# One token block instead of two goes through the row gather, and ScalarE's share of that work is issued later

## The chip, the cores and the metric

The kernel runs on one core of one Trainium2 chip. The metric is the device time of one execution in microseconds (us). TensorE (PE in the profile), VectorE (DVE), ScalarE (ACT) and GpSimd (POOL) each run their own instructions strictly in order, and SyncE (SP) issues most of the DMAs, in order too. An instruction waits for the semaphores of what it needs; everything behind it on its engine waits with it. GpSimd issues the indirect DMAs and the DMAs that add to their target.

## The reference, cut to what matters

2048 tokens of 512 numbers are normalised, and the result is the input plus two branches: a Fourier mix over both axes, and a layer of 4096 small experts. For each token and each of 32 heads the second branch picks 2 experts out of 4096 (by two rounds of top-2 over scores against the keys), weighs them by a softmax, and sums the value rows:

```python
x = A_x
xn = _layernorm(x, axis=-1)
...
g = _softmax(top_s, axis=-1)
ue = u[top_e]
ve = v[top_e]
act = _gelu(jnp.einsum("nd,nhkd->nhk", xf, ue))
out = jnp.einsum("nhk,nhk,nhkd->nd", g, act, ve)
...
return x + _A_ref(xn, ...) + _B_ref(xn, ...)
```

So a token has 64 slots (32 heads, 2 experts each). A slot costs one dot product of the token with a row of `u`, a gelu, a product with the gate, and one scaled row of `v`.

## The kernel before

The tokens are 16 blocks of 128. A first part of the program does the Fourier mix, all the scores and the routing; it ends at about 450 us, with the expert numbers `eix` and gates `gts` of the last `NS` blocks on the chip. What follows is the expert stage, and the change lies there. Two ways of doing a block run side by side in it.

**Dense blocks** (`NB` = 16 − `NS` of them). All 4096 experts are computed for the block. `u_part(b, cg)` makes 128 x 512 products with `u` in PSUM (tile `z`, 48 matmuls, two banks of the tag `pb` in turn), and ScalarE takes each out with a gelu into `act` (L936). `g_mm` builds on TensorE the matrix `g` of gates (zero for experts that were not picked) out of one-hot tiles `L` and `R` that VectorE writes (L959, L964, L967). `w_part` multiplies `act` by `g` on VectorE into a tile `w` (L979), ScalarE rounds it to a 16-bit half (L983) and VectorE takes the rest as a second half (L984). `v_part` multiplies the halves with `v` (L991), eight steps `cg` of 12 matmuls for one block, and `finish` adds the sum to `y` on VectorE (L1006), where the Fourier branch and the input already are (`add_x`), and stores it.

**Row blocks** (the last `NS`). For each slot an indirect DMA fetches a row of `u` and a row of `v` for each of the 128 tokens into one tile `ga` (`fetch`, L1017, 512 KB). `dot` multiplies the `u` half by the token on VectorE and sums (L1037); ScalarE does the gelu and the gate on the 128 sums (tile `za`, L1038 and L1039) and, in `gain`, scales the `v` half (L1045); GpSimd adds it to the block's sum `ov` (L1046). There are `NS` x 64 slots, in order.

The loop is over the dense blocks: eight steps of `v_part(b)`, then eight steps of `u_part(b+2)` while there is such a block. I call one such pair a period: the V phase and the U phase. `w_part` and `g_mm` of the next blocks are placed at fixed steps by the small tables `vw`, `vg`, `uw` and `ug`. After every step from block 1 on, `pick` issues the next pieces of the row work, spread evenly: `picks` is the list dot, gain, dot, gain, and so on, over `turns` steps. In the same steps `paced` issues two streams of checks that the first part could not finish: `fit` (ScalarE takes the sum of magnitudes of a tile) and `compare` or `compare_w` (a DMA, several subtractions on VectorE called `diff`, and two sums of magnitudes on ScalarE called `judge`). A function appended to `later` is issued one step on. `verdict` reduces the checks over the partitions with two `PARTITION_ALL_REDUCE` on GpSimd and sets a flag that decides whether a slower path runs afterwards.

Within a phase the order on each engine is that of issue, as the recording layer schedules it; `follow` and `hold` only place an instruction behind a matmul in that order, they add no wait.

Of the kernel before, what the change touches and what calls it, by code (L numbers as in the profile page):

```python
# [19 lines left out]
P = 128  # L20
# [12 lines left out]
NS = 2  # L33
# [3 lines left out]
def tile_fnet_peer(ctx, tc, x, ca, cb, c5, wt, wf, wr, wq, kt, ut, vn, uv, out):  # L37
# [515 lines left out]
    def part_b(safe, stS, stP, stE, xt, u_sb, cmp_p):  # L553
# [161 lines left out]
        def compare(n, at=None):  # L715
# [188 lines left out]
        BT = [blk_tiles(b) for b in range(2)]  # L904
# [4 lines left out]
        BUFS = 3  # L909
        AHEAD = BUFS - 1  # L910
# [63 lines left out]
        def w_part(b, tg):  # L974
            act, _ = ACT[b]
            ts = slice(tg * TG, (tg + 1) * TG)
            p = GP.pop((b, tg))
            w = bp.tile([P, NC, TG], F32, tag="w", name=f"w{b}_{tg}", bufs=WB)
            nc.vector.scalar_tensor_tensor(w, act[:, :, ts], fw,  # L979
                                           p.rearrange("p h (n c) -> p c (h n)", c=NC),  # L980
                                           op0=ALU.mult, op1=ALU.mult)
            w16 = parts(b)[:, :, ts]
            nc.scalar.activation(w16[..., 0], w, AF.Copy)  # L983
            nc.vector.tensor_tensor(w16[..., 1], w, w16[..., 0], op=ALU.subtract)  # L984
# [36 lines left out]
        def dot(n, s):  # L1021
            if s == 0:
                b = NB + n
                xs = bp.tile([P, 2 * D], F32, tag="ga", name=f"xs_{n}", bufs=BUFS)[:, :D]
                T["x"] = pc(f"px{n}")
                T["z"] = bp.tile([P, N], F32, tag="za", name=f"za{n}", bufs=1)
                T["o"] = o = bp.tile([P, D], F32, tag="ov", name=f"ov{n}", bufs=1)
                nc.sync.dma_start(xs, x[b // 4, b % 4])
                nc.sync.dma_start(o, y_d[b])
                nc.gpsimd.dma_start(o, x[b // 4, b % 4], accum_op=ALU.add)  # L1030
                norm(T["x"], xs, b)
                if n == 0:
                    for _ in range(AHEAD):
                        fetch()
            t = T[n, s][:, :D]
            z = T["z"][:, s:s + 1]
            nc.vector.scalar_tensor_tensor(t, t, 1.0, T["x"], op0=ALU.mult, op1=ALU.mult, accum_out=z)  # L1037
            nc.scalar.activation(z, z, AF.Gelu_apprx_tanh)  # L1038
            nc.scalar.activation(z, z, AF.Copy, scale=gts[:, n].rearrange("p k h -> p (k h)")[:, s:s + 1])  # L1039
            fetch()  # L1040

        def gain(n, s):
            o = T["o"]
            t = T.pop((n, s))[:, D:]
            nc.scalar.activation(t, t, AF.Copy, scale=T["z"][:, s:s + 1])  # L1045
            nc.gpsimd.tensor_tensor(o, o, t, op=ALU.add)  # L1046
            if s == N - 1:
                b = NB + n
                nc.sync.dma_start(out[b * P:(b + 1) * P], o)
# [17 lines left out]
        def compare_w(n):  # L1067
# [35 lines left out]
            later.append(lambda mm: nc.scalar.activation(f, f, AF.Abs, accum_out=chk[:, n:n + 1]))  # L1103

        def fit(n):

            if n < NW:
                t = bp.tile([P, 2 * D], F32, tag="w", name=f"fit{n}", bufs=WB)
                nc.sync.dma_start(t.rearrange("p (h k) -> p h k", h=2), wq[1 + n // 4, n % 4 // 2, n % 2])
                later.append(lambda mm: nc.scalar.activation(t, t, AF.Abs, accum_out=fits[:, n:n + 1]))  # L1110
# [5 lines left out]
            nc.scalar.activation(t, src, AF.Abs, accum_out=fits[:, n:n + 1])  # L1116
# [75 lines left out]
        for cg in range(8):  # L1192
            u_part(1, cg)
            if cg % 2 == 0:
                w_part(0, cg // 2)
# [4 lines left out]
        last = list(range(V2, 16))  # L1200
        for b in range(NB):
            pv = pc(f"v{b}")
            if b + 2 < NB:
                vw, vg, uw, ug = {0: 0, 4: 1}, {2: 2, 6: 3}, {0: 2, 4: 3}, {2: 0, 6: 1}
            else:
                vw, vg = {0: 0, 2: 1, 4: 2, 6: 3}, {0: 2, 3: 3}
            for cg in range(8):
# [3 lines left out]
                mm = v_part(b, pv, cg)  # L1211
                if b + 1 < NB and cg in vw:
                    w_part(b + 1, vw[cg])
# [21 lines left out]
            for cg in range(8 if b + 2 < NB else 0):  # L1235
                mm = u_part(b + 2, cg)
                if cg in uw:
                    w_part(b + 1, uw[cg])
# [150 lines left out]
```

## Time and profile before

| what | us |
|---|---|
| median of 3 runs (1172.79 to 1180.67) | 1174.48 |
| the profiled execution | 1180.07 |
| its span | 1178.2 |
| expert stage up to the first V phase | 450.0 to 503.7 |
| twelve periods (V phase of block b, U phase of block b+2) | 503.7 to 1114.0 |
| V phases of blocks 12 and 13, and the end | 1114.0 to 1178.2 |
| VectorE, ScalarE, GpSimd busy in the whole span | 984.5, 731.5, 658.1 |
| TensorE busy in the whole span | 1085.4 |

A period starts with the first `v` matmul of its block. Those stand in the trace's order in time at 503.74, 554.02, 602.21, 649.16, 701.17, 749.39, 796.99, 847.99, 905.16, 960.14, 1014.21, 1062.20 and 1113.97 us. In a group's row the last column is the time in which the engine sat idle just ahead of such instructions, with what ended the wait behind the arrow.

### The profile page before, as it was taken

The page shows a single profiled execution, that of the slowest core. Times are in us where ns is not written, and L with a number is a line of the kernel's source. Part 1 is how long each engine was busy: PE and PEld are TensorE (multiplying, and loading weights), DVE is VectorE, ACT ScalarE, POOL GpSimd, SP SyncE. Part 2 cuts the span into 40 slices and gives each one's busy share as a digit, 9 for nine tenths or more (in the row PEclk, how much of TensorE's full clock was granted, in tenths as well). Part 3 has the DMA queues.
Part 4 walks back from the last instruction along what each step waited for, and adds up shares of the span by engine and source line. Part 5 has one row for each costly group of instructions (what it writes and reads, how often), then busy time and mean ns, then how long its engine had stood idle before and what let it go on. Part 6 is the DMA issues. An engine that isn't in the chain of part 4 may idle for free. (4 is left out here: it accounts for less than half of the span.)

```text
span 1178.2 us, 28689 instructions
## 1 busy us (share of the span) xinstructions
PE 1085.4 (92%) x11070; PEld 710.4 (60%) x11070; DVE 984.5 (84%) x2886; ACT 731.5 (62%) x1429; POOL 658.1 (56%) x570
## 2 busy tenths in 40 slices
PE   6899999999999999999999989999879797999885
PEld 4355555444444447958668676786748576786732
DVE  7878888797987998889898978789688987889861
ACT  3575567787877874457666657666555665675550
POOL 0021748779878771246557556666565655566542
PEclk9799999999999999999999999999998998999998
DMA  8265236253542421345765656666654656565541
GB/s 309 77 218 177 92 124 214 93 180 124 166 161 85 144 97 60 103 139 171 214 201 169 215 182 209 185 191 199 198 169 167 194 164 204 168 203 173 162 117 48
DMA packets 82418, 190.44 MB, mean 162 GB/s; under 512 B 10070, under 2 KB 26845, under 8 KB 82272
## 3 DMA queue, kind: packets, MB, share of 16 engines
q1 hardware_dynamic: 61378, 117.20, 29.7%
q0 software_dynamic: 20736, 71.31, 20.4%
q8 instruction: 88, 1.44, 0.5%
q14 instruction: 58, 0.48, 0.1%
q10 hardware_dynamic: 158, 0.01, 0.0%
HBM read 174.53 MB, written 13.96 MB: 160 GB/s over the span
## 5 line engine op out<-in xcount | busy, mean ns | idle before, releaser
L933 PE MATMUL z<-xb,u 128*128 128x128 f16 x5376 | 322.8, 224 | 49.7 <-ACT act L936 47.2
L933 PEld LDWEIGHTS <-u 128*128 128x128 f16 x5376 | 315.6, 100 | 54.5 <-issue 49.0
L790 PE MATMUL s<-m,xq 128*128 128x512 f16 x1536 | 339.1, 379 | 0.9 <-ACT ss L795 0.9
L1046 POOL TENSOR_TENSOR ov<-ov,ga 128x512 f32<-128x512 f32 x128 | 199.6, 1559 | 208.6 <-ACT ga L1045 180.6
L991 PE MATMUL v<-v,act 128*128 128x512 f16 x1344 | 300.5, 380 | 2.1 <-DVE y L1006 2.1
L790 PEld LDWEIGHTS <-xq 128*128 128x128 f16 x1536 | 148.3, 98 | 172.4 <-issue 1.4
L991 PEld LDWEIGHTS <-act 128*128 128x128 f16 x1344 | 128.8, 98 | 149.5 <-issue 4.6
L1017 POOL DMA_INDIRECT ga<-in_uv_dram,eix x128 | 163.5, 1278 | 64.4 <-POOL ov L1046 32.5
L959 DVE TENSOR_TENSOR L<-io_lam,cmp 128x2048 f16<-128x2048 f16 x112 | 155.0, 1384 | 43.2 <-PE g L969 41.1
L798 DVE MAX8 vals<-ss 128x8 f32<-128x64 f32 x1024 | 152.5, 216 | 16.2 <-ACT ss L795 16.1
L1037 DVE SCALAR_TENSOR_TENSOR ga<-ga,px 128x512 f32<-128x512 f32 x128 | 86.3, 678 | 41.2 <-DMA ga<-in_uv_dram,eix 39.6
L936 ACT ACTIVATE act<-z,scl 128x512 f32<-128x512 f32 x112 | 75.5, 678 | 66.0 <-PE z L933 60.8
L802 DVE FIND_INDEX8 idx<-vals,ss 128x8 uint16<-128x256 f32 x256 | 107.2, 419 | 0.0
L983 ACT ACTIVATE act<-w 128x1024 f16<-128x1024 f32 x56 | 75.2, 1350 | 43.0 <-DVE w L979 35.0
L1038 ACT ACTIVATE za<-za 128x1 f32<-128x1 f32 x128 | 25.1, 196 | 119.6 <-DVE ga L1037 112.7
L1045 ACT ACTIVATE ga<-ga,za 128x512 f32<-128x512 f32 x128 | 91.9, 718 | 7.8 <-ACT za L1039 0.4
L795 ACT ACTIVATE ss<-s,wsc 128x512 f32<-128x512 f32 x112 | 75.2, 679 | 28.2 <-PE s L790 15.2
L984 DVE TENSOR_TENSOR act<-w,act 128x1024 f16<-128x1024 f32 x56 | 76.9, 1373 | 15.7 <-ACT act L983 9.9
L773 ACT ACTIVATE cx<-cx 128x896 f32<-128x896 f32 x64 | 60.7, 948 | 43.9 <-DVE cx L753 10.4
L747 POOL TENSOR_TENSOR cx<-cx 128x512 f32<-128x512 f32 (+2 forms) x56 | 61.9, 1124 | 29.0 <-DMA cx<-in_cb_dram 27.0
L979 DVE SCALAR_TENSOR_TENSOR w<-act,scl,g 128x1024 f32<-128x1024 f32 x56 | 70.5, 1271 | 2.7 <-POOL v L612 2.0
L967 DVE TENSOR_TENSOR R<-R,cmp 128x512 f16<-128x512 f16 x112 | 68.9, 615 | 1.2
(276 smaller groups left out, 1379.7 us busy)
## 6 DMA issues: line engine op xcount, KB each, us to landing
cx<-in_cb_dram SPq DMA_DIRECT2D x64, 448.0 KB
wq<-in_wq_dram SPq DMA_DIRECT2D x32, 512.0 KB
fit<-in_wq_dram SPq DMA_DIRECT2D x28, 512.0 KB
uv<-in_ut_dram SPq DMA_DIRECT2D x16, 512.0 KB
uv<-in_vn_dram SPq DMA_DIRECT2D x16, 512.0 KB
xq<-in_x_dram SPq DMA_DIRECT2D x8, 512.0 KB
xt_d<-xq SPq DMA_DIRECT2D x16, 256.0 KB
cx<-in_ca_dram SPq DMA_DIRECT2D x64, 64.0 KB
```

The lines of the kernel that those rows point to most:

```text
L790: mm = nc.tensor.matmul(ps, xt[i][:, l, kd, :], m[:, r, kd, :], start=(n == 0), stop=(n == 3 * KD - 1))
L798: nc.vector.max(vals[:, i, w, :, h], s[:, g, :])
L802: nc.vector.max_index(idx[:, i, w].rearrange("p k h -> p (k h)"), vals[:, i, w, 0:2].rearrange("p k h -> p (k h)"), s[:, w * HC:g + 1, :]. ...
L933: mm = nc.tensor.matmul(p[:, cc * P:(cc + 1) * P], ug[:, l, c % 2, kd, :], xb[:, r, kd, :], start=(n == 0), stop=(n == 3 * KD - 1))
L936: nc.scalar.activation(act[:, cg * 4:cg * 4 + 4, :].rearrange("p c n -> p (c n)"), p, AF.Gelu_apprx_tanh, scale=zsc)
L959: nc.vector.tensor_tensor(L.rearrange("p t (l two) -> p t l two", two=2), io_lam.rearrange("p (l two) -> p l two", two=2).unsqueeze(1).to_ ...
L984: nc.vector.tensor_tensor(w16[..., 1], w, w16[..., 0], op=ALU.subtract)
L991: mm = nc.tensor.matmul(pv, w16[:, c, :, l], vg[:, r, c % 2, :], start=(c == 0 and k == 0), stop=(c == NC - 1 and k == 2))
L1017: nc.gpsimd.indirect_dma_start(out=t, out_offset=None, in_=uv, in_offset=bass.IndirectOffsetOnAxis(ap=eix[:, n].rearrange("p k h -> p (k h ...
L1037: nc.vector.scalar_tensor_tensor(t, t, 1.0, T["x"], op0=ALU.mult, op1=ALU.mult, accum_out=z)
L1045: nc.scalar.activation(t, t, AF.Copy, scale=T["z"][:, s:s + 1])
L1046: nc.gpsimd.tensor_tensor(o, o, t, op=ALU.add)
```

## The change

Five things change together.

1. `NS` goes from 2 to 1. Fifteen blocks are dense, one is done by rows: 64 slots instead of 128, over 212 steps instead of 196. There are thirteen periods instead of twelve. The streams of checks are the same work over 106 instead of 98 steps each.
2. The row work is cut elsewhere. `dot` is now the VectorE instruction alone; `gain` holds gelu, gate, scaling and sum of a slot and then the next `fetch`, and stands one slot behind in `picks`: dot 0, dot 1, gain 0, dot 2, gain 1. The tile `ga` has four buffers instead of three. The load for the row block's tokens moves to a `w` buffer, and `xb_1`, the token tile of the second dense block, to a `ga` buffer; all other `xb` share one buffer instead of two. The scratch for GpSimd's DMA descriptors is halved.
3. `w_part` now returns the two halves' instructions (L983 and L984 of before), and the loop issues them one step later.
4. The checks' ScalarE sums, and the subtractions of `compare`, are issued one or two steps later than before (`after(k, f)`).
5. Two of the fixed steps move by one: `w_part(b+1, 3)` from step 4 to step 3 of the U phase, and `g_mm(b+1, 2)` from step 0 to step 1 in the last periods.

```diff
-NS = 2
+NS = 1
...
             if at is None:
-                def work(mm):
-                    hold(diff, mm)
-                    later.append(lambda mm: hold(judge, mm))
-
-                later.append(work)
+                def work():
+                    diff()
+                    after(2, judge)
+
+                after(2, work)
...
-            xb = ap[0].tile([P, 2, KD, P], F16, tag="xb", name=f"xb_{b}", bufs=2)
+            if b == 1:
+                xb = bp.tile([P, 2, 2, KD, P], F16, tag="ga", name="xb_1", bufs=BUFS)[:, 0]
+            else:
+                xb = ap[0].tile([P, 2, KD, P], F16, tag="xb", name=f"xb_{b}", bufs=1)
...
-        BUFS = 3
-        AHEAD = BUFS - 1
+        BUFS = 4
...
-            nc.scalar.activation(w16[..., 0], w, AF.Copy)
-            nc.vector.tensor_tensor(w16[..., 1], w, w16[..., 0], op=ALU.subtract)
+            def halves(mm=None):
+                i = nc.scalar.activation(w16[..., 0], w, AF.Copy)
+                if mm is not None:
+                    follow(i.ins, mm)
+                nc.vector.tensor_tensor(w16[..., 1], w, w16[..., 0], op=ALU.subtract)
+
+            return halves
...
+            t = T[n, s][:, :D]
+            nc.vector.scalar_tensor_tensor(t, t, 1.0, T["x"], op0=ALU.mult, op1=ALU.mult,
+                                           accum_out=T["z", n][:, s:s + 1])
+
+        def gain(n, s):
...
             nc.scalar.activation(z, z, AF.Gelu_apprx_tanh)
             nc.scalar.activation(z, z, AF.Copy, scale=gts[:, n].rearrange("p k h -> p (k h)")[:, s:s + 1])
+            t = T.pop((n, s))[:, D:]
+            nc.scalar.activation(t, t, AF.Copy, scale=z)
+            nc.gpsimd.tensor_tensor(o, o, t, op=ALU.add)
             fetch()
...
-        picks = [] if safe else [lambda f=f, n=n, s=s: f(n, s) for n, s in rows for f in (dot, gain)]
+        picks = []
+        for i in range(0 if safe else len(rows) + 1):
+            picks += [lambda f=f, k=k: f(*k) for f, k in ((dot, rows[i:i + 1]), (gain, rows[i - 1:i] if i else [])) for k in k]
...
+        def after(k, f):
+            later.append(lambda mm: hold(f, mm) if k == 1 else after(k - 1, f))
...
-                vw, vg, uw, ug = {0: 0, 4: 1}, {2: 2, 6: 3}, {0: 2, 4: 3}, {2: 0, 6: 1}
+                vw, vg, uw, ug = {0: 0, 4: 1}, {2: 2, 6: 3}, {0: 2, 3: 3}, {2: 0, 6: 1}
             else:
-                vw, vg = {0: 0, 2: 1, 4: 2, 6: 3}, {0: 2, 3: 3}
+                vw, vg = {0: 0, 2: 1, 4: 2, 6: 3}, {1: 2, 3: 3}
...
-    nc = bacc.Bacc("TRN2", target_bir_lowering=False, num_devices=1, dynamic_dma_scratch_size=4096)
+    nc = bacc.Bacc("TRN2", target_bir_lowering=False, num_devices=1, dynamic_dma_scratch_size=2048)
```

The orders that follow have their own line numbers: in the changed kernel the gelu out of `z` is L938, the one-hot tiles L961, L966 and L969, `w_part` L981 with its halves L988 and L991, `dot` L1042, the three ScalarE instructions of `gain` L1053, L1054 and L1056, its sum L1057, the fetch L1026, and `finish` L1015.

**Place 1: ScalarE at the start of the U phase of block 9.** `z9_0` is the first gelu of that phase, `ga1_9` slot 9 of the second row block, `cx36` a check's tile, `fit37` a check. Before:

```order
L773 ACTIVATE cx36_12719,sums_90<-cx36_12719 128x896
L774 ACTIVATE cx36_12719,sums_90<-cx36_12719 128x128
L1038 ACTIVATE za1_12202<-za1_12202 128x1
L1116 ACTIVATE fit37_13138,sums_90<-u9_128 128x1024
L1039 ACTIVATE za1_12202<-za1_12202,gts_98 128x1
L1045 ACTIVATE ga1_9_12705<-ga1_9_12705,za1_12202 128x512
L936 ACTIVATE act9_12689<-z9_0_12813,scl_99 128x512
L983 ACTIVATE act8_11877<-w8_3_13127 128x32x32
L936 ACTIVATE act9_12689<-z9_1_12869,scl_99 128x512
```

The same place now, with slots 33 and 34 of the only row block (the last row is slot 34's gelu; slot 33's stands just ahead of the first row):

```order
L938 ACTIVATE act9_12384<-z9_0_12497,scl_99 128x512
L1054 ACTIVATE za0_7231<-za0_7231,gts_98 128x1
L1056 ACTIVATE ga0_33_12000<-ga0_33_12000,za0_7231 128x512
L988 ACTIVATE act8_11624<-w8_2_12547 128x32x32
L938 ACTIVATE act9_12384<-z9_1_12556,scl_99 128x512
L1129 ACTIVATE fit36_12549,sums_90<-u8_127 128x1024
L938 ACTIVATE act9_12384<-z9_2_12615,scl_99 128x512
L773 ACTIVATE cx35_12492,sums_90<-cx35_12492 128x896
L938 ACTIVATE act9_12384<-z9_3_12705,scl_99 128x512
L774 ACTIVATE cx35_12492,sums_90<-cx35_12492 128x128
L1053 ACTIVATE za0_7231<-za0_7231 128x1
```

Before, a whole check, slot 9's three instructions and a `fit` stand between the end of the V phase and `z9_0`; now the phase's gelus stand further forward, and slot 34 begins behind the fourth of them.

**Place 2: VectorE at the same time.** `y7` is `finish` of block 7, which needs the last matmul of the V phase, `w8_3` a product with the gates, `L0` to `L2` and `R0` to `R2` the one-hot tiles. Before:

```order
L753 TENSOR_TENSOR cx36_12719<-cx36_12719 1x128
L959 TENSOR_TENSOR L1_5869<-io_lam_70,cmp9_12693 128x2048
L761 COPY cx36_12719<-cx36_12719 1x128
L1037 SCALAR_TENSOR_TENSOR ga1_9_12705,za1_12202<-ga1_9_12705,px1_12201 128x512
L1006 SCALAR_TENSOR_TENSOR y7_12699<-v7_12546,scl_99,y7_12699 128x512
L964 TENSOR_TENSOR R1_5870<-io_c_71,cmp9_12693 128x512
L979 SCALAR_TENSOR_TENSOR w8_3_13127<-act8_11877,scl_99,g8_3_12736 128x1024
```

And now:

```order
L1042 SCALAR_TENSOR_TENSOR ga0_34_12203,za0_7231<-ga0_34_12203,px0_7230 128x512
L981 SCALAR_TENSOR_TENSOR w8_2_12547<-act8_11624,scl_99,g8_2_12306 128x1024
L966 TENSOR_TENSOR R0_5868<-io_c_71,cmp9_12388 128x512
L961 TENSOR_TENSOR L1_5869<-io_lam_70,cmp9_12388 128x2048
L969 TENSOR_TENSOR R0_5868<-R0_5868,cmp9_12388 128x512
L1015 SCALAR_TENSOR_TENSOR y7_12396<-v7_12261,scl_99,y7_12396 128x512
L966 TENSOR_TENSOR R1_5870<-io_c_71,cmp9_12388 128x512
```

Before, the end of the check `cx36` and slot 9's dot, which ScalarE's row above needs ahead of `z9_0`, stand right ahead of `y7`. Now the nearest dot ahead of `y7` is slot 34's, which ScalarE needs only behind `z9_3`, and `w8_2` is ahead of `y7` too.

**Place 3: GpSimd at the end of the program.** `y12`, `y13` and `y14` are the sums of dense blocks, `fr` the two reductions of `verdict`, `ISA` the switch between GpSimd's programs. Before:

```order
L1134 ISA
L1134 ISA fr_16901<-fa_16900 128x2
L1046 ISA
L1046 TENSOR_TENSOR ov1_12203<-ov1_12203,ga1_60_16668 128x512
L1000 DMA y13_16897<-in_x_dram 128x512
L1017 DMA ga1_63_16816<-in_uv_dram,eix_97 128x1024
L1046 TENSOR_TENSOR ov1_12203<-ov1_12203,ga1_61_16747 128x512
L1135 ISA
L1135 ISA fr_16901<-sums_90 128x70
L1046 ISA
L1046 TENSOR_TENSOR ov1_12203<-ov1_12203,ga1_62_16766 128x512
L1046 TENSOR_TENSOR ov1_12203<-ov1_12203,ga1_63_16816 128x512
```

And now:

```order
L1026 DMA ga0_63_16759<-in_uv_dram,eix_97 128x1024
L1057 TENSOR_TENSOR ov0_7454<-ov0_7454,ga0_60_16185 128x512
L1009 DMA y13_16984<-in_x_dram 128x512
L1057 TENSOR_TENSOR ov0_7454<-ov0_7454,ga0_61_16340 128x512
L1150 ISA
L1150 ISA fr_17129<-fa_17128 128x2
L1057 ISA
L1057 TENSOR_TENSOR ov0_7454<-ov0_7454,ga0_62_16558 128x512
L1009 DMA y14_17125<-in_x_dram 128x512
L1057 TENSOR_TENSOR ov0_7454<-ov0_7454,ga0_63_16759 128x512
L1151 ISA
L1151 ISA fr_17129<-sums_90 128x70
```

Before, the last fetch and three sums stand behind the first reduction, and the last two sums behind the second. Now the last fetch stands ahead of the first reduction, two sums stand behind that one, and none behind the second.

More of the change, by code (lines that the diff above doesn't have):

```diff
@@ L908, in part_b @@
         WB = 4
-        BUFS = 3
-        AHEAD = BUFS - 1
+        BUFS = 4
+        BT = [blk_tiles(b) for b in range(2)]
         NB = NT if safe else NT - NS
@@ L1027, in dot @@
+                if n == 0:
+                    for _ in range(BUFS):
+                        fetch()
+            t = T[n, s][:, :D]
+            nc.vector.scalar_tensor_tensor(t, t, 1.0, T["x"], op0=ALU.mult, op1=ALU.mult,
+                                           accum_out=T["z", n][:, s:s + 1])
+        def gain(n, s):
+            b = NB + n
+            if s == 0:
                 T["o"] = o = bp.tile([P, D], F32, tag="ov", name=f"ov{n}", bufs=1)
-                nc.sync.dma_start(xs, x[b // 4, b % 4])
@@ L1029, in dot @@
                 nc.sync.dma_start(o, y_d[b])
                 nc.gpsimd.dma_start(o, x[b // 4, b % 4], accum_op=ALU.add)
[L1031 to L1037, printed above, removed]
+            o = T["o"]
+            z = T["z", n][:, s:s + 1]
             nc.scalar.activation(z, z, AF.Gelu_apprx_tanh)
@@ L1102, in compare_w @@
             f = t.rearrange("p k e -> p (k e)")[:, P - half * ri:]
-            later.append(lambda mm: nc.scalar.activation(f, f, AF.Abs, accum_out=chk[:, n:n + 1]))
+            after(2, lambda: nc.scalar.activation(f, f, AF.Abs, accum_out=chk[:, n:n + 1]))
         def fit(n):
@@ L1236, in part_b @@
                 mm = u_part(b + 2, cg)
+                for f in split:
+                    f(mm)
+                split = []
                 if cg in uw:
-                    w_part(b + 1, uw[cg])
+                    split = [w_part(b + 1, uw[cg])]
                 if cg in ug:
```

25 lines of the change are left out of this document (12 added, 13 removed).

## The prediction

> **What bounds the kernel now.** I read the busy time by stages first (start and end, length, then busy us of each engine with the count of instructions, TensorE's granted clock, DMA share, GB/s), then the waits of the expert stage, then the timeline around the worst of them.
>
> ```profile
> span 1178.2 us, 28689 instructions
> core 0: us, PE busy (x) PEld busy (x) DVE busy (x) ACT busy (x) POOL busy (x), PEclk, DMA share, GB/s
> 503.70:1114.00 610.30, 561.85 (x7357) 423.76 (x7354) 532.74 (x831) 374.83 (x769) 364.93 (x257) 0.97 0.60 185
> 602.20:649.20 47.00, 45.73 (x616) 34.33 (x613) 42.46 (x69) 32.16 (x66) 31.49 (x22) 1.00 0.65 202
> 848.00:905.20 57.20, 48.32 (x615) 36.69 (x613) 49.22 (x78) 32.27 (x68) 34.52 (x24) 0.91 0.54 172
> ```
>
> The twelve periods take 610.3 us, 50.85 each. The best one takes 47.00 with TensorE busy for 45.73; that is its floor, since the same matmuls stand in every period. A bad one takes 57.20 with the clock at 0.91. So 610.3 − 12 x 45.73 = 61.5 us are lost to waits and clock. VectorE is close behind: 532.74 / 12 = 44.4 per period.
>
> ```profile
> ACT za L1038 <- DVE ga L1037: 88.6, 53, 4.7
> PE z L933 <- ACT act L936: 47.2, 16, 8.8
> ACT act L983 <- DVE w L979: 31.9, 20, 5.4
> DVE ga L1037 <- DMA ga<-in_uv_dram,eix: 22.0, 8, 6.7
> ```
>
> These rows give the total, the times and the longest wait. Of the 61.5 us, 47.2 are TensorE waiting for ScalarE to empty a bank of `z`; the other 14.3 are small waits and the slower clock behind long ones. ScalarE's own largest wait is for a dot (88.6), and some dots wait for their gather (22.0). The timeline of the worst wait (start, length, instruction, idle time ahead of it):
>
> ```profile
> 634.96 10.88 PE L933 MATMUL z<-xb,u 128*128 128x128 f16 x192 [1.27 <-ACT act L936]
> 877.88 0.20 ACT L1038 ACTIVATE za<-za 128x1 f32<-128x1 f32 x1 [4.33 <-DVE ga L1037]
> 880.96 0.95 ACT L773 ACTIVATE cx<-cx 128x896 f32<-128x896 f32 x1 [1.75 <-DVE cx L761]
> 882.29 1.04 ACT L1116 ACTIVATE fit<-u 128x1024 f32<-128x1024 f16 x1
> 884.32 0.67 ACT L936 ACTIVATE act<-z,scl 128x512 f32<-128x512 f32 x1
> 885.04 5.28 PE L933 MATMUL z<-xb,u 128*128 128x128 f16 x48 [8.78 <-ACT act L936]
> ```
>
> ScalarE is not out of time. It stands 4.33 us at a gelu whose dot VectorE has not done, then 1.75 at a check, then does a `fit`, and only then takes `z` out. TensorE has filled both banks and idles for 8.78; its next 48 matmuls take 5.28, against 48 x 10.88 / 192 = 2.72 at full clock. So the loss is an order problem: ScalarE's queue holds instructions that depend on fresh VectorE work ahead of the gelu on which TensorE depends.
>
> **The change part by part.** The costs per slot are these (busy us of the group, mean ns, idle time):
>
> ```profile
> L1037 DVE SCALAR_TENSOR_TENSOR ga<-ga,px 128x512 f32<-128x512 f32 x120 | 81.0, 678 | 23.6 <-DMA ga<-in_uv_dram,eix 22.0 <-POOL ov L1046 1.5
> L1038 ACT ACTIVATE za<-za 128x1 f32<-128x1 f32 x120 | 23.5, 196 | 95.5 <-DVE ga L1037 88.6 <-DVE R L967 3.5 <-issue 2.2
> L1039 ACT ACTIVATE za<-za,gts 128x1 f32<-128x1 f32 x120 | 35.1, 292 | 3.4
> L1045 ACT ACTIVATE ga<-ga,za 128x512 f32<-128x512 f32 x120 | 86.1, 718 | 7.0
> L1046 POOL TENSOR_TENSOR ov<-ov,ga 128x512 f32<-128x512 f32 x120 | 189.1, 1575 | 186.0 <-ACT ga L1045 171.6 <-ACT za L1038 6.9 <-DMA ov<-in_x_dram 4.3
> L959 DVE TENSOR_TENSOR L<-io_lam,cmp 128x2048 f16<-128x2048 f16 x100 | 140.3, 1403 | 37.8 <-PE g L969 35.7 <-ACT cmp L697 2.0
> 883.98 1.21 DVE L959 TENSOR_TENSOR L<-io_lam,cmp 128x2048 f16<-128x2048 f16 x1
> 892.93 2.96 DVE L959 TENSOR_TENSOR L<-io_lam,cmp 128x2048 f16<-128x2048 f16 x1
> ```
>
> *The period.* 64 slots over 13 periods is 4.9 per period, where 120 over 12 were 10. VectorE loses 5.1 x 0.678 = 3.4 us per period, ScalarE 5.1 x (0.196 + 0.292 + 0.718) = 6.2, GpSimd 5.1 x 1.575 = 8.0. VectorE also works faster beside less of GpSimd's work: L959 takes 1.21 in one place and 2.96 in another, 1.403 in the mean, so (1.403 − 1.21) x 100 / 12 = 1.6 per period, of which about half goes. VectorE comes to 44.4 − 3.4 − 0.8 = 40.2 under a floor of 45.7. It gets 5.5 us of slack where it had 1.3.
>
> The Trainium skill (SBUF — State Buffer, "Who interferes with whom") states that VectorE with two SBUF inputs and a GpSimd instruction that reads SBUF take turns on one port pair, each for a whole instruction. By that rule, which the 2.96 beside 1.21 agrees with, up to 94 of GpSimd's 189.1 us, 7.8 per period, could stop blocking VectorE instead of my 0.8; the sum would then stand at its lower end, 1153.6, with no stall left.
>
> The new order cuts the dependence as well: at place 1 slot 33's multiply and scaling, whose dot is long done, stand ahead of `z9_1`, the checks behind `z9_1` and `z9_2`, and slot 34's gelu behind `z9_3`. Its product `w8_2` has a whole step before ScalarE wants it. The gathers get more time: a fetch is issued 5 picks ahead of its dot at 128 picks / 212 steps, 8.3 steps or some 24 us, where it was 4 picks at 256 / 196, 3.1 steps or some 9 us.
>
> ```profile
> 1154.30 1.12 POOL L1017 DMA_INDIRECT ga<-in_uv_dram,eix  x1 [0.30 <-issue]
> 1159.88 0.69 DVE L1037 SCALAR_TENSOR_TENSOR ga<-ga,px 128x512 f32<-128x512 f32 x1 [17.60 <-DMA ga<-in_uv_dram,eix]
> ```
>
> A gather lands about 5.6 us after issue, so the 22.0 us of waits for gathers should go. What stays per period, s, I put at 0.5: below the 1.27 of the best period before, which still had ten slots; ends 0 and 1.5. The stage: 13 x (45.7 + 0.5) − 610.3 = 600.6 − 610.3 = **−9.7**, ends −16.2 and +3.3. In other words the extra dense block costs 45.7 and the stalls pay for it.
>
> *The last two V phases.*
>
> ```profile
> 1114.00:1141.70 27.70, 22.77 (x163) 10.95 (x161) 24.74 (x50) 17.81 (x37) 13.51 (x11) 1.00 0.51 143
> 1129.36 0.55 PE L969 MATMUL g<-R,L 128*128 128x32 f16 x16 [1.88 <-DVE R L967]
> 1141.73 22.57 PE L991 MATMUL v<-v,act 128*128 128x512 f16 x96 [2.10 <-DVE y L1006]
> ```
>
> They last from 1113.97 to 1141.73 + 22.57 = 1164.30, 50.3 us, of which TensorE works 22.77 + 22.57 = 45.3. VectorE was late (1.88 and 2.10, busy 24.74 of 27.70) and has half the dots now; I keep 1.4 of the 5.0 lost: 46.7, **−3.6**, ends −5.0 and 0.
>
> *The end.*
>
> ```profile
> 1144.66 0.41 POOL L1134 PARTITION_ALL_REDUCE fr<-fa  x1 [6.83 <-issue]
> 1151.75 1.26 POOL L1046 TENSOR_TENSOR ov<-ov,ga 128x512 f32<-128x512 f32 x1 [6.68 <-issue]
> 1152.96 1.04 POOL L1000 DMA_DIRECT2D y<-in_x_dram  x1
> 1155.42 1.31 POOL L1046 TENSOR_TENSOR ov<-ov,ga 128x512 f32<-128x512 f32 x1
> 1162.57 0.60 POOL L1135 PARTITION_ALL_REDUCE fr<-sums  x1 [5.83 <-ACT ga L1045]
> 1163.21 0.23 DVE L1138 TENSOR_SCALAR fr<-fr,wsc 1x28 f32<-1x28 f32 x1 [2.63 <-POOL fr L1135]
> 1164.67 0.75 DVE L1006 SCALAR_TENSOR_TENSOR y<-v,scl,y 128x512 f32<-128x512 f32 x1
> 1165.45 0.34 SPq L1007 DMA_DIRECT2D out_dram<-y  x1
> 1170.04 2.59 POOL L1046 TENSOR_TENSOR ov<-ov,ga 128x512 f32<-128x512 f32 x2 [6.86 <-issue]
> 1172.65 0.34 SPq L1049 DMA_DIRECT2D out_dram<-ov  x1
> ```
>
> From TensorE's last matmul to the end are 1178.2 − 1164.3 = 13.9 us. The last store of `y` goes out 1.15 after TensorE, but two sums of `ov` stand behind the second reduction and the switch of 6.86 ahead of them, so their store goes out only at 1172.65, and the end is 5.55 behind it. Place 3 takes those sums away from there. With V the end of block 13's V phase, GpSimd does the first reduction by V + 4 (it was 3.4 after 1141.7), then the switch 6.7, sum 1.3, `y14` 1.0, sum 1.3, switch 6.8, reduction 0.6: V + 21.7, and VectorE's verdict 1.5 more, V + 23.2. TensorE ends at V + 0.8 + 22.6 = V + 23.4, so the last `y` decides: 1.15 + 5.55 = 6.7. As the verdict is that close ahead of `finish` on VectorE, I take 7.2: **−6.7**, ends −7.2 and 0.
>
> *At nothing:* one `xb` buffer (free when a U phase ends, and 22.57 us of V phase cover a load of at most the gather's 5.6); `xb_1` in a `ga` buffer (one load before 503.7, 5.6 once if uncovered); the smaller scratch (64 fetches in 601 us are 9.4 us apart and land in 5.6, so about one is open at a time; if one had to wait for the one before, that is 5.6 out of its 24). The halves a step later, and the product and `g_mm` moved by a step, are the same instructions, and the halves are still four steps or more ahead of the `v` matmuls that read them; if that cover is gone, a V phase starts late by about the 2.10 at 1141.73, which is inside my ends for s.
>
> Sum: −9.7 − 3.6 − 6.7 = −20.0; the profiled run took 1180.07, hence **1160 us**. That run is 5.6 above the median 1174.48. I do not subtract that again: the new stage is built from its floor, so a stall more or less in the old run drops out.
>
> **The rivals.** *Slower: the added block is paid, the stalls stay.* ScalarE's wait moves from the dot to the halves: at place 1 the half of `w8_2` (L988) stands ahead of `z9_1` and needs VectorE's product, and L983 waited for L979 already (31.9 us, up to 5.4). If VectorE still runs late, TensorE waits at `z` as before: 13 x 50.85 − 610.3 = +50.8, less 10.3 at the end: 1180.1 + 40.5 = 1221. It decides once s is over 0.5 + (1186.2 − 1160.1) / 13 = 2.5, half of today's 5.1. For it: VectorE's 42.46 in the best period shows how little it takes. Against: that period lost only 1.27 with VectorE at 42.46, and VectorE now has 2.3 less than that. *Part stays:* s from 1.5 to 2.5, 1173 to 1186. *The end is not shortened:* the first reduction comes later than V + 8, as the checks run later, and the verdict or a sum ends last: up to +6.7, 1167. *The order does nothing:* only the removed slots count; that is s near 2, in the second case.
>
> **How the numbers follow.** 1% is about what a measurement of this kernel can tell from no change: faster is below 1162.7, slower above 1186.2. The forecast (s up to 1.5, 1152 to 1173) has 0.60: 0.50 below 1162.7, 0.10 above. Part stays 0.18, the end 0.07, both within 1%; slower 0.15. So 0.50, 0.35, 0.15. The range runs from 1148 (s = 0, both ends at their best, 1151.7, and most of the 5.6 not in the stalls) to 1186, and leaves out the slower case.
>
> **What would show it.** Thirteen periods of 46 to 47 us with the clock at 1.00; PE z <- ACT act far below 47.2; no waits of dots for gathers; VectorE near 40 per period; the last DMA issue a store of `y`, about 7 us before the end. It is wrong if PE z <- ACT act stays above 25 us (then look for L988 waiting on L981), if VectorE's busy share rises, or if a store of `ov` or the verdict's flag ends last.

## The result, and the profile after

The changed kernel takes 1160.38 us (median of 4 runs, 1159.16 to 1161.23) beside 1175.07 for the kernel before on the same chip: ratio 0.987, 95% interval 0.983 to 0.990. It is faster by 1.3%, and the forecast was 1160. The profiled execution took 1159.16 with a span of 1157.4.

First the busy time by stages of the changed kernel, with the columns of the same view before. The rows are the first period, two single periods, periods 2 to 13 together, and what lies behind them, cut where block 13's V phase ends.

```profile
502.30:555.80 53.50, 47.39 (x636) 35.02 (x633) 44.95 (x60) 24.15 (x34) 14.06 (x9) 0.97 0.31 92
555.80:601.30 45.50, 45.50 (x615) 34.18 (x612) 38.71 (x66) 24.64 (x48) 16.34 (x10) 1.00 0.47 143
601.30:646.90 45.60, 45.60 (x616) 34.26 (x614) 37.00 (x62) 24.16 (x45) 15.03 (x11) 1.00 0.43 130
555.80:1102.20 546.40, 546.40 (x7337) 410.44 (x7334) 431.27 (x686) 294.64 (x568) 185.65 (x128) 1.00 0.46 139
1102.20:1126.00 23.80, 23.18 (x165) 11.14 (x162) 18.77 (x33) 11.86 (x21) 5.41 (x5) 1.00 0.24 57
1126.00:1157.40 31.40, 20.48 (x95) 9.13 (x94) 6.18 (x31) 4.09 (x10) 4.58 (x5) 0.91 0.16 45
```

In twelve of the thirteen periods TensorE is busy for 546.40 of 546.40 us with the clock at 1.00: 45.53 per period and no wait at all. VectorE has 431.27 / 12 = 35.9 per period and GpSimd 15.5. The only loss of the stage is in the first period, 7.9 us. TensorE's waits from 495 us on:

```profile
PE g L971 <- DVE R L969: 6.7, 3, 4.2
PE v L1000 <- DVE act L991: 1.1, 1, 1.1
```

The row that led before, `z` waiting for ScalarE (47.2 us), is gone. Two of the three waits for `R` lie in the first period. The timeline there shows VectorE's one-hots beside the last four fills of `v` on GpSimd:

```profile
504.35 2.13 POOL L612 TENSOR_TENSOR v<-uv,v 128x1024 f16<-128x1024 f32 x1 [1.67 <-ACT uv L611]
504.43 2.33 DVE L969 TENSOR_TENSOR R<-R,cmp 128x512 f16<-128x512 f16 x1
509.02 6.87 POOL L612 TENSOR_TENSOR v<-uv,v 128x1024 f16<-128x1024 f32 x3 [2.55 <-ACT uv L611]
513.84 3.14 DVE L961 TENSOR_TENSOR L<-io_lam,cmp 128x2048 f16<-128x2048 f16 x1
516.90 0.41 DVE L969 TENSOR_TENSOR R<-R,cmp 128x512 f16<-128x512 f16 x1
517.36 0.59 PE L971 MATMUL g<-R,L 128*128 128x32 f16 x16 [4.20 <-DVE R L969]
```

L969 takes 0.41 alone and 2.33 beside GpSimd's fill of `v`. The end of the program (start, length, instruction, idle time ahead of it):

```profile
1130.70 0.41 POOL L1150 PARTITION_ALL_REDUCE fr<-fa  x1 [6.08 <-ACT ga L1056]
1138.43 1.25 POOL L1057 TENSOR_TENSOR ov<-ov,ga 128x512 f32<-128x512 f32 x1 [7.33 <-issue]
1148.04 0.60 POOL L1151 PARTITION_ALL_REDUCE fr<-sums  x1 [6.04 <-issue]
1150.31 0.75 DVE L1015 SCALAR_TENSOR_TENSOR y<-v,scl,y 128x512 f32<-128x512 f32 x1
1151.24 0.34 SPq L1016 DMA_DIRECT2D out_dram<-y  x1
```

TensorE ends at 1127.16 + 20.46 = 1147.62 (its row is in the table of the third experiment). The last store is one of `y`, as forecast, but the second reduction runs only at 1148.04, so the verdict and with it `finish` are late: the end is 9.8 us behind TensorE.

The profiled runs side by side, by where the stages begin and end (first `v` matmul; first `v` matmul behind the last `z`; last `v` matmul; span):

| us | before | after | difference | forecast |
|---|---|---|---|---|
| up to the first V phase | 503.7 | 502.4 | −1.4 | 0 |
| periods (12; 13) | 610.2 | 599.8 | −10.4 | −9.7 |
| last two V phases | 50.3 | 45.4 | −4.9 | −3.6 |
| behind TensorE | 13.9 | 9.8 | −4.1 | −6.7 |
| span | 1178.2 | 1157.4 | −20.8 | −20.0 |

### The profile page after: what moved, and what is told of

Read it like the earlier page. It is cut to its first block, busy times and chain, and to the rows that moved or that the text cites. A ratio compares the mean times of both kernels' runs of the same rounds, so it can differ in the third digit from the quotient of the medians.

```text
span 1157.4 us, 29244 instructions
## 1 busy us (share of the span) xinstructions
PE 1111.0 (96%) x11681; PEld 730.1 (63%) x11681; DVE 924.8 (80%) x2790; ACT 670.4 (58%) x1250; POOL 482.4 (42%) x442
## 3 DMA queue, kind: packets, MB, share of 16 engines
q1 hardware_dynamic: 61522, 117.30, 30.4%
q0 software_dynamic: 11520, 37.75, 11.8%
## 4 chain that ended last, share of the span: by engine, by line
PE 71%; DVE 12%; POOL 8%; issue 3%; ACT 2%; DMA 2%; SPq 0%; POOLq 0%; DVEq 0%; ACTq 0%
PE z L935 27%; PE v L1000 23%; PE s L790 12%; PE g L971 4%; DVE vals L798 2%; POOL wq L168 2%; DVE idx L802 2%; POOL wq L167 2%; PE p L368 2%; POOL cx L747 1%; POOL u L612 1%; DMA cx<-in_cb_dram 1%; PE m L146 1%; DVE L L961 1%; DVE ft L345 1%
## 5 line engine op out<-in xcount | busy, mean ns | idle before, releaser
L935 PE MATMUL z<-xb,u 128*128 128x128 f16 x5760 | 330.6, 219 | 2.4 <-DMA xb<-xt_d 2.4
L935 PEld LDWEIGHTS <-u 128*128 128x128 f16 x5760 | 324.5, 98 | 5.7 <-DMA xb<-xt_d 2.6
L1000 PE MATMUL v<-v,act 128*128 128x512 f16 x1440 | 321.3, 380 | 1.2 <-DVE act L991 1.1
L1057 POOL TENSOR_TENSOR ov<-ov,ga 128x512 f32<-128x512 f32 x64 | 96.0, 1500 | 401.0 <-ACT ga L1056 345.5
L961 DVE TENSOR_TENSOR L<-io_lam,cmp 128x2048 f16<-128x2048 f16 x120 | 157.2, 1310 | 112.5 <-PE g L971 79.0
L1000 PEld LDWEIGHTS <-act 128*128 128x128 f16 x1440 | 137.7, 98 | 159.1 <-issue 1.7
L938 ACT ACTIVATE act<-z,scl 128x512 f32<-128x512 f32 x120 | 81.9, 684 | 174.9 <-PE z L935 174.7
L1026 POOL DMA_INDIRECT ga<-in_uv_dram,eix x64 | 93.7, 1463 | 32.3 <-POOL ov L1057 18.3
L991 DVE TENSOR_TENSOR act<-w,act 128x1024 f16<-128x1024 f32 x60 | 81.0, 1350 | 19.2 <-ACT act L988 17.5
L988 ACT ACTIVATE act<-w 128x1024 f16<-128x1024 f32 x60 | 80.9, 1348 | 26.5 <-DVE w L981 26.4
L981 DVE SCALAR_TENSOR_TENSOR w<-act,scl,g 128x1024 f32<-128x1024 f32 x60 | 76.2, 1273 | 0.1
L971 PEld LDWEIGHTS <-L 128*128 128x128 f16 x1920 | 56.0, 96 | 15.5 <-issue 8.7
L971 PE MATMUL g<-R,L 128*128 128x32 f16 x1920 | 57.9, 176 | 8.0 <-DVE R L969 8.0
L969 DVE TENSOR_TENSOR R<-R,cmp 128x512 f16<-128x512 f16 x120 | 62.3, 519 | 1.8
L168 POOL TENSOR_TENSOR wq<-wq,wh 128x1024 f16<-128x1024 f32 x26 | 55.4, 2130 | 18.9 <-ACT wq L165 17.9
```

The source lines that it names most:

```text
L935: mm = nc.tensor.matmul(p[:, cc * P:(cc + 1) * P], ug[:, l, c % 2, kd, :], xb[:, r, kd, :], start=(n == 0), stop=(n == 3 * KD - 1))
L938: nc.scalar.activation(act[:, cg * 4:cg * 4 + 4, :].rearrange("p c n -> p (c n)"), p, AF.Gelu_apprx_tanh, scale=zsc)
L961: nc.vector.tensor_tensor(L.rearrange("p t (l two) -> p t l two", two=2), io_lam.rearrange("p (l two) -> p l two", two=2).unsqueeze(1).to_ ...
L971: i = nc.tensor.matmul(p[:, hf, t * NC:(t + 1) * NC], L[:, t, :], R[:, t, :], start=True, stop=True)
L988: i = nc.scalar.activation(w16[..., 0], w, AF.Copy)
L1000: mm = nc.tensor.matmul(pv, w16[:, c, :, l], vg[:, r, c % 2, :], start=(c == 0 and k == 0), stop=(c == NC - 1 and k == 2))
```

## The experiments

Two questions were open: whether the fewer slots or the new order ended the stalls, and what a period needs to stall at all. Every kernel ran with the kernel before on the same chip; ratios are to that. The last four columns are of each one's profiled execution (us), which is one of its runs and can lie some us from the median: that of experiment 3 took 1161.21, that of experiment 12 took 1172.28. "z waits" is TensorE's time waiting for ScalarE to empty a bank of `z`, from 495 us on.

| kernel | median us | ratio, 95% interval | z waits | periods | last two V | behind TensorE |
|---|---|---|---|---|---|---|
| before (two blocks) | 1175 to 1179 | 1 | 47.2 | 610.2 | 50.3 | 13.9 |
| changed (one block) | 1160.4 | 0.987, 0.983 to 0.990 | 0 | 599.8 | 45.4 | 9.8 |
| 1: one block, old order | 1158.9 | 0.986, 0.983 to 0.988 | 2.9 | 601.2 | 48.7 | 6.6 |
| 2: two blocks, new order | 1159.2 | 0.986, 0.983 to 0.989 | 8.8 | 586.8 | 52.8 | 14.7 |
| 3: changed, reductions last | 1157.6 | 0.984, 0.981 to 0.987 | 0 | 600.0 | 47.8 | 6.6 |
| 4: changed, old dot and gain | 1157.5 | 0.985, 0.982 to 0.987 | 0.6 | 602.1 | 45.7 | 6.5 |
| 5: as 1, dots x3 | 1165.6 | 0.989, 0.985 to 0.993 | 10.1 | 606.9 | 48.1 | 6.5 |
| 6: changed, dots x3 | 1166.4 | 0.989, 0.985 to 0.993 | 0 | 600.1 | 50.5 | 10.6 |
| 7: as 2, reductions last | 1154.2 | 0.981, 0.976 to 0.986 | 11.8 | 587.6 | 51.7 | 6.5 |
| 8: as 2, old dot and gain | 1164.0 | 0.988, 0.984 to 0.991 | 30.4 | 592.0 | 49.5 | 14.1 |
| 9: as 1, dots x4 | 1183.6 | 1.004, 1.002 to 1.007 | 23.7 | 621.8 | 45.7 | 10.2 |
| 10: before, four buffers | 1174.5 | 0.997, 0.996 to 0.999 | 37.0 | 603.7 | 50.3 | 14.8 |
| 11: as 2, checks as before | 1171.8 | 0.996, 0.994 to 0.999 | 34.2 | 597.6 | 56.9 | 11.8 |
| 12: as 2, halves as before | 1179.6 | 1.002, 1.000 to 1.005 | 33.7 | 600.8 | 51.8 | 14.4 |

The old order is row work, halves and checks as before; the new order is as in the changed kernel.

**1. One block, old order.** In the kernel before:

```diff
-NS = 2
+NS = 1
```

> The kernel before with NS = 1 and nothing else: 64 row slots in the old order. Theory A (the order of ScalarE's queue makes the stalls): ScalarE still stands at fresh dots and checks ahead of the gelu out of z, so TensorE waits for z remain, 12 to 35 us over the thirteen periods, s 1.5 to 3, time 1172 to 1195. Theory B (the slack on VectorE alone ends the stalls): waits for z under 5 us, time 1156 to 1166, the same as the changed kernel.

Theory A falls, B holds: 1158.85. TensorE's and ScalarE's waits from 495 us on:

```profile
PE z L933 <- ACT act L936: 2.9, 2, 2.5
ACT za L1038 <- DVE ga L1037: 37.6, 27, 4.1
```

ScalarE still stands at fresh dots 27 times, for 37.6 us; in the periods alone it is 31.6 us, where the kernel before had 88.6. Its waits for the products are longer (57.1 us from 495 us on, 31.9 before), and yet it reaches `z` in time. The order that I had read as the cause does almost no harm with one row block.

**2. Two blocks, new order.** In the changed kernel:

```diff
-NS = 1
+NS = 2
```

> The changed kernel with NS = 2: 128 row slots, twelve periods, all of the new order. Theory A: the waits for z are gone or under 10 us in all; twelve periods of 45.5 to 46.5 and the same start: one period less than the changed kernel and two switches more at the end, 1115 to 1130. Theory B: VectorE has 44 us of work in a period of 45.5, so it runs late again, waits for z of 30 us and more, periods of 49 to 51, 1155 to 1180.

Neither holds whole. The waits for `z` are under 10 us, as A had it, but the periods take 48.9 instead of A's 45.5 to 46.5, and the time is 1159.2, in B's range. TensorE waits for VectorE in another place now, and ScalarE for the products (last row, for later):

```profile
PE g L971 <- DVE w L981: 16.8, 6, 8.0
PE z L935 <- ACT act L938: 8.8, 10, 1.8
PE g L971 <- DVE R L969: 8.5, 5, 3.4
ACT act L988 <- DVE w L981: 51.7, 18, 13.3
```

The new order protects `z`, and VectorE's lateness goes on to the `g` matmuls, most of them in the V phases (25.3 us in the first and third row; 4.4 of it is in the first period, where the changed kernel waits as well). The periods still gain 23 us on the kernel before. So each half of the change alone is worth about 1.4%, and together they are worth no more: with one block nothing is left for the order to save, and the dense block costs TensorE the 45.5 us that the second row block did not.

**3. Both reductions behind the last sum.** In the changed kernel:

```diff
-                    verdict()
...
+            elif b + 1 == NB:
+                made = nc.cur_bb.bb.instructions
+                first = len(made)
+                verdict()
+                for i in made[first:]:
+                    if i.engine == mybir.EngineType.Pool:
+                        follow(i, T["add"])
             finish(b, pv)
```

`T["add"]` is the last sum of `ov`.

> The changed kernel with both reductions of the verdict behind the last sum of ov on GpSimd, side by side. In the changed kernel the second reduction runs at 1148.04, 0.4 us behind TensorE's last matmul, because two more switches of GpSimd's programs stand between the first and the second. If the verdict is what ends last, the second reduction should now end at about 1142 to 1143, the last y is stored about 1.2 us after TensorE's end, and the time falls by 2 to 3 us to 1157.5 to 1158.5. If the last store of y would be late anyway (TensorE, or y's own load), the time stays within 0.7 us of 1160.4.

1157.57, in the expected range; the ratio's interval overlaps that of the changed kernel, so the time alone would not settle it. The profiles do: TensorE's end to the span's end is 6.6 us, where the changed kernel needs 9.8. The first row is TensorE's last in the changed kernel, the others are of this run:

```profile
1127.16 20.46 PE L1000 MATMUL v<-v,act 128*128 128x512 f16 x94 [1.14 <-DVE act L991]
```

```profile
1130.80 22.05 PE L1000 MATMUL v<-v,act 128*128 128x512 f16 x94 [1.14 <-DVE act L991]
1145.50 0.68 POOL L1151 PARTITION_ALL_REDUCE fr<-sums  x1
1152.89 0.75 DVE L1015 SCALAR_TENSOR_TENSOR y<-v,scl,y 128x512 f32<-128x512 f32 x1 [5.01 <-PE v L1000]
```

The second reduction ends 6.7 us ahead of TensorE's last matmul, and `finish` waits for TensorE alone. In experiments 1 and 4 no sum stands between the two reductions either (the second ends at 1126.74 and 1134.65, long before TensorE), and their ends take 6.6 and 6.5. So the 3 us at the end of the changed kernel come from where the two reductions fall among the sums.

**4. Old dot and gain.** The changed kernel with this alone undone:

```diff
+            nc.vector.scalar_tensor_tensor(t, t, 1.0, T["x"], op0=ALU.mult, op1=ALU.mult, accum_out=z)
+            nc.scalar.activation(z, z, AF.Gelu_apprx_tanh)
+            nc.scalar.activation(z, z, AF.Copy, scale=gts[:, n].rearrange("p k h -> p (k h)")[:, s:s + 1])
+            fetch()
...
-        picks = []
-        for i in range(0 if safe else len(rows) + 1):
-            picks += [lambda f=f, k=k: f(*k) for f, k in ((dot, rows[i:i + 1]), (gain, rows[i - 1:i] if i else [])) for k in k]
+        picks = [] if safe else [lambda f=f, n=n, s=s: f(n, s) for n, s in rows for f in (dot, gain)]
```

> The changed kernel with the row work cut as before: gelu, gate and fetch again with the dot, gain only scales and adds, dot and gain of one slot side by side; one block, four buffers, halves and checks as in the changed kernel. Theory A, with this part as its core: ScalarE waits at fresh dots again (30 us and more in all), TensorE waits 8 to 25 us for z, 1166 to 1182. Theory A without this part, or theory B: within 3 us of 1160.4, TensorE's waits for z under 3 us.

One fetch less runs ahead, as in the kernel before. The time is 1157.45 with 0.6 us of waits for `z`. ScalarE's waits from 495 us on have this row, which the changed kernel has not:

```profile
ACT za L1044 <- DVE ga L1043: 82.7, 33, 6.4
```

Theory A's premise came true (30 us and more at fresh dots), and what it was to lead to did not: the lag of a slot is not needed with one block.

**5 and 6. More work for VectorE.** Ahead of every dot, in the kernel of experiment 1 and in the changed kernel:

```diff
+            for _ in range(2):
+                nc.vector.scalar_tensor_tensor(T["x"], t, 0.0, T["x"], op0=ALU.mult, op1=ALU.add,
+                                               accum_out=T["z"][:, s:s + 1])
```

> One block in the old order (the kernel of the first experiment) with two extra instructions of the dot's form ahead of every dot; they add zero times the gathered row to the token tile, so the result is the same. VectorE gets 2 x 64 x 0.68 = 87 us more, 6.7 per period, and comes from 35.4 to about 42.1, near the 44.4 of the kernel before; GpSimd, ScalarE and the gathers have the work of one block. Theory B (VectorE's slack decides): the waits for z come back, 15 to 45 us, 1168 to 1195. Rival C (what a second row block costs on GpSimd, ScalarE and in gathers makes the stalls, not VectorE's load): waits for z under 6 us, 1157 to 1163.

> The changed kernel with the same two extra instructions ahead of every dot: VectorE from 35.9 to about 42.6 per period. Theory D (the new order protects the z banks, but VectorE's lateness goes on to other waits): waits for z under 8 us, waits of the g matmuls for VectorE 8 to 25 us, 1163 to 1178, and less than the run with the old order by 5 us or more. Rival C: within 3 us of 1160.4. Rival E (order is worth nothing): the same time and the same waits for z as the run with the old order, within 3 us.

In the old order the waits for `z` come back, but only 10.1 us, and 1165.6 lies between the ranges of B and C as well:

```profile
PE z L933 <- ACT act L936: 10.1, 13, 1.5
```

In the new order there are none, and the periods take 600.1 instead of 606.9, as long as in the changed kernel. The totals are equal (1165.6 and 1166.4), since the new order's run loses those 7 us and 3 more ahead of the first V phase, in the last V phases and at the end. So D is right that the new order protects `z`, but the lateness does not go on to `g`: those waits are 6.7 us, as in the changed kernel, and not 8 to 25. D is also wrong about the difference of 5 us; E is right about the total and wrong about the waits. With this load on VectorE the order is worth 7 us in the periods even with one block.

**9. Three extra instructions, old order.** As 5, with `range(3)`.

> One block in the old order with three extra instructions ahead of every dot: VectorE is asked for 35.4 + 3 x 3.35 = 45.4 us per period, no less than in the kernel before (44.4). Theory B (VectorE's load in the old order is all that the stalls need): the waits for z rise steeply from the 10.1 of two extra instructions to 35 to 60 us, 1185 to 1215. Rival C (the second row block's gathers, GpSimd and ScalarE work are needed as well): waits for z 10 to 25 us, 1168 to 1182.

The waits are C's (23.7), the time lies between the two ranges. The periods of this kernel by engine:

```profile
502.20:1123.90 621.70, 596.87 (x7964) 447.18 (x7961) 591.13 (x1108) 323.16 (x602) 200.16 (x138) 1.00 0.44 133
```

VectorE is busy for 591.13 of 621.70 us, 45.5 per period: more than in the kernel before (44.4). Yet the periods lose 621.8 − 13 x 45.53 = 30 us, where the kernel before lost 610.2 − 12 x 45.53 = 64. VectorE's load alone makes about half of those stalls. What makes the other half is not shown. The second row block's other work is left for it: its gathers, its share of GpSimd and of ScalarE.

**10. Four buffers in the kernel before.**

```diff
-            xb = ap[0].tile([P, 2, KD, P], F16, tag="xb", name=f"xb_{b}", bufs=2)
+            if b == 1:
+                xb = bp.tile([P, 2, 2, KD, P], F16, tag="ga", name="xb_1", bufs=BUFS)[:, 0]
+            else:
+                xb = ap[0].tile([P, 2, KD, P], F16, tag="xb", name=f"xb_{b}", bufs=1)
...
-        BUFS = 3
+        BUFS = 4
...
```

> The kernel before with four ga buffers instead of three, and what makes room for them (one xb buffer, xb_1 in a ga buffer, xs in a w buffer, half the scratch); order and NS = 2 as before. If late gathers (22.0 us of VectorE's waits) feed the stalls: those waits fall under 8 us, the waits for z from 47 to under 35, the ratio to before 0.985 to 0.995. If not: waits for z 40 us and more, ratio 0.995 to 1.005.

No dot waits for a gather any more, and the waits for `z` go from 47.2 to 37.0, between the two forecasts. The profiled runs took 1180.07 and 1172.50, so a part of these 10 us can be the difference between two runs. The ratio is 0.997, in the range of "if not", with its interval (0.996 to 0.999) below 1: the four buffers with what makes room for them are worth 0.1 to 0.4%, so late gathers are a small part of the stalls at most. GpSimd's and ScalarE's shares were not tried apart.

**8, 11 and 12. Parts of the order, with two blocks.** Experiment 2 with one part undone each: 8 has the edit of experiment 4; 11 and 12 have these:

```diff
-                def work():
-                    diff()
-                    after(2, judge)
-
-                after(2, work)
+                def work(mm):
+                    hold(diff, mm)
+                    later.append(lambda mm: hold(judge, mm))
+
+                later.append(work)
...
-                    split = [w_part(b + 1, vw[cg])]
+                    w_part(b + 1, vw[cg])()
```

The first is 11, which undoes the delays of `compare_w` and `fit` too; the second is 12, which does the same for `uw`.

> NS = 2, halves and checks late as in the changed kernel, but gelu, gate and fetch with the dot again. If the lag of a slot is the part of the order that frees z at NS = 2 (place 1): waits for z from 8.8 back to 25 to 45 us, 1166 to 1182. If the late halves and checks do it: waits for z under 14 us, within 5 us of 1159.

> NS = 2 in the new order, but the checks' sums and subtractions issued as soon as before. If the late checks are a part of what frees ScalarE at place 1: waits for z from 8.8 to 20 us and more, 5 us or more above the 1159 of NS = 2 in the new order. If not: waits for z under 14 us and within 4 us of 1159.

> NS = 2 in the new order, but ScalarE's and VectorE's halves issued in the same step as the product. If the late halves are a part of it: waits for z from 8.8 to 20 us and more, 5 us or more above 1159. If not: waits for z under 14 us and within 4 us of 1159.

Each part is needed: undone, each brings the waits for `z` to 30 us and more. In time the lag of a slot is worth the least (1164.0, five us; the ratio's interval overlaps that of experiment 2), the checks' delay 1%, the halves' delay 1.6%, all that the order gains; the shares do not add. Experiment 12's profiled run took 1172.28, 7 us under its median; its ScalarE and TensorE rows:

```profile
ACT act L988 <- DVE w L981: 122.8, 42, 10.1
PE z L935 <- ACT act L938: 33.7, 14, 5.5
```

A half that is issued right behind its product makes ScalarE wait 122.8 us for VectorE, 51.7 in experiment 2. The longest wait of ScalarE in experiments 8 and 11 for something other than TensorE:

```profile
ACT za L1044 <- DVE ga L1043: 159.0, 69, 6.4
ACT fit L1123 <- DMA fit<-in_wq_dram: 67.4, 25, 7.2
```

By the times, the instruction in ScalarE's queue that matters most is the half, not the dot: experiment 8 has the longer wait, at the dots, and loses 5 us where experiment 12 loses 20. And the checks that are issued early in experiment 11 hold ScalarE for their own load (67.4 us) as well as for VectorE's subtractions (42.7 in the largest row).

**7. Two blocks, new order, reductions last.** Experiments 2 and 3 together.

> NS = 2 in the new order with both reductions behind the last sum of ov. In the run of NS = 2 in the new order TensorE ended at 1142.5 and the span at 1157.2, since the last sum of ov (1150.28) stood behind the second reduction and a switch. Now the last y should be stored about 1.2 us behind TensorE's end and the end be 6.7 behind it: 8 us less, 1151, faster than both kernels; 1148 to 1155. If something else holds the end (the verdict, the last gather), less than 4 us come off.

1154.15, within the range, and the lowest median here: 1.9% under the kernel before (1.4 to 2.4%). The step from experiment 2 is 5 us by the medians and 8.2 by the profiles' ends; its four runs go from 1150.49 to 1161.01, and its interval overlaps that of experiment 2. Its end:

```profile
1127.88 2.60 POOL L1057 TENSOR_TENSOR ov<-ov,ga 128x512 f32<-128x512 f32 x2 [1.00 <-ACT za L1053]
1136.43 0.41 POOL L1150 PARTITION_ALL_REDUCE fr<-fa  x1 [5.94 <-issue]
1136.76 0.68 POOL L1151 PARTITION_ALL_REDUCE fr<-sums  x1
1142.12 0.75 DVE L1015 SCALAR_TENSOR_TENSOR y<-v,scl,y 128x512 f32<-128x512 f32 x1 [2.98 <-PE v L1000]
1142.90 0.34 SPq L1016 DMA_DIRECT2D out_dram<-y  x1
```

The reductions are done 4.6 us ahead of TensorE's end, and `finish` waits for TensorE alone. Experiment 2 paid 14.7 us there because its last sum stood behind the second reduction.

## Why the prediction was right, and where it was not

**The bound and the sum.** TensorE's floor decides the time, and thirteen floors replace twelve stalled periods: −10.4 measured, −9.7 forecast. The floor is 45.53, not 45.7, and the rest s is 599.8 / 13 − 45.53 = 0.6 per period (forecast 0.5). The size is right by luck: all of it lies in the first period, for another reason than I gave (the one-hots late beside the fills of `v`), and the other twelve have s = 0. The first period takes 50.3 to 52.1 us in the old order (the kernel before, experiments 1, 5, 9 and 10) and 53.4 to 55.0 in the new one (the changed kernel, 2, 3, 4, 6, 7 and 8), so the new order costs 1 us or more there. Luck is in the sum too: the start, the periods and the last V phases came out 1.4, 0.7 and 1.3 better than forecast and the end 2.6 worse. The start lies between 500.6 and 505.0 in these runs, so its 1.4 is no effect that can be told from chance.

**"The loss is an order problem": the step that failed.** The profile showed ScalarE's queue behind fresh VectorE work, and I let the new order and the slack share the credit. With one block and no load added the order isn't needed at all: experiment 1 has s = 601.2 / 13 − 45.53 = 0.7 in the old order. The rival "the order does nothing", priced at s near 2, had its premise come true there, and its price was wrong. With two blocks the order matters (experiments 2, 8, 11, 12), and the halves more than the dots. The number survived since both readings give the same thirteen floors; as far as the order goes, that is luck.

**VectorE's slack: mis-sized.** VectorE's work comes to 35.9 per period in periods 2 to 13, not 40.2: 8.5 less than before, where I had 4.2. The one-hots in periods 2 to 13:

```profile
L961 DVE TENSOR_TENSOR L<-io_lam,cmp 128x2048 f16<-128x2048 f16 x97 | 127.3, 1312 | 95.0 <-PE g L971 66.3 <-ACT cmp L697 28.5
L966 DVE TENSOR_TENSOR R<-io_c,cmp 128x512 f16<-128x512 f16 x96 | 48.5, 505 | 0.0
L969 DVE TENSOR_TENSOR R<-R,cmp 128x512 f16<-128x512 f16 x97 | 47.0, 484 | 1.7
```

The kernel before has 1403 ns for the first, and for the other two these, over its twelve periods:

```profile
L964 DVE TENSOR_TENSOR R<-io_c,cmp 128x512 f16<-128x512 f16 x99 | 62.7, 633 | 0.0
L967 DVE TENSOR_TENSOR R<-R,cmp 128x512 f16<-128x512 f16 x99 | 61.5, 621 | 1.2
```

Eight of each per period save 8 x (0.091 + 0.128 + 0.137) = 2.8 us, and I had counted 0.8 from L959 alone. The dots save 3.5, the five largest groups of the checks' subtractions 1.3. The missing row block is what shortens the one-hots, not the order: the means of the two 128 x 512 rows are 500 and 569 ns with one block in the old order (experiment 1), 656 and 693 with two in the new one (experiment 2). By the rule of the Trainium skill (SBUF — State Buffer, "Who interferes with whom") I had estimated 7.8 as the most; the rows agree with its direction, and lie between my price and that bound. The lower end of the sum that went with it, 1153.6, was not reached, as the first period and the end hold the rest.

**Gathers:** no dot in the periods waits for one, as forecast. **Last V phases:** −4.9 for −3.6; the wait ahead of the last phase is 1.1 where it was 2.10.

**The end: mis-sized.** With V at 1126.0 the second reduction was forecast to end at V + 21.7 and ended at V + 22.6; TensorE was forecast at V + 23.4 and ended at V + 21.6. TensorE's last phase took 20.46 with the clock at 1.00, and I had taken its length from the kernel before, 22.57 with the clock at 0.92. The two errors of 0.9 and 1.8 turned the order of the two around: the verdict, which I had 0.2 ahead, is behind, so that −6.7 became −4.1. One of my own signs of being wrong came up with it: the last store waits for the verdict. Experiment 3 shows the 6.6 us that the forecast had in mind.

**At nothing:** the edits to `xb`, `xb_1`, scratch and tables cost nothing that the profile shows; experiment 4 keeps them and has 45.7 for its last V phases and 0.6 us of waits for `z`, and experiment 10 has the first three in the kernel before, at a ratio of 0.997. The two moved steps were not tried by themselves. **The slower rival** did not come with one block. Its mechanism is real with two: experiment 12 is the one where ScalarE's wait moves to the halves. **The 5.6 us:** the kernel before had medians of 1175.1 to 1179.5 in the comparisons here (1178.8 over 31 runs), so its profiled run, 1180.07, was 1 to 5 us above typical.

## What to carry to other kernels

When an engine waits for another's queue, two cures compete: give the late engine slack, or put the urgent instruction ahead of what depends on it. Try each alone before adding their gains; here each was worth 1.4%, and both together no more. When the bound engine gets more work to buy the slack, ask whether the order alone would have done, and look at the program's end by itself: by the medians three us (one block) or five (two) lay there in the place of two reductions. How long an engine waits in all is a poor guide to what it costs: 82.7 us of ScalarE's waits at dots cost TensorE 0.6 with one block.

## What was not expected of the hardware

Two `PARTITION_ALL_REDUCE` side by side take 0.41 and 0.68 us with no gap, while GpSimd idles for 5.8 to 7.3 us at each turn between a reduction and a sum in the ends shown here. And VectorE's one-hots of 128 x 512 run at 0.41 us alone and at up to 2.3 us beside GpSimd (for L967 of the kernel before, 0.42 on average where it overlaps no sum of GpSimd and 1.07 where it does), so taking work from GpSimd gave VectorE nearly as much time (2.8 us per period) as the dots that were taken from VectorE itself (3.5). The dots themselves take 0.68 in both cases.
